# Opening of a silu MLP kernel: x's contraction tile 1 loaded behind the third warm-up matmul, first contraction tile multiplied by halves of the rows

## The chip, the cores and the metric

The kernel runs on one core of a Trainium2 chip. The metric is the device time of one execution in microseconds (us), where lower is better. The profile beside it was taken of one execution, and its span counts from the program's first instruction to its last.

## The reference

`x` is 2048 x 640, `w1` is 640 x 1728 and `w2` is 1728 x 640, all bf16.

```python
def reference(x, w1, w2):
    h = jnp.einsum("bsd,df->bsf", x, w1)
    h = _silu(h)
    out = jnp.einsum("bsf,fd->bsd", h, w2)
    return out
```

## The kernel before

The work is written out by hand as one list of operations. Each operation names its engine and the operations that it depends on; each engine runs its own operations in the order of that list, and a dependency on another engine or on a DMA becomes a semaphore wait in front of the instruction. Nothing is reordered by a planner.

TensorE (PE) needs x with its contraction dimension on the partitions. So x is held as `xT_sb`, five contraction tiles (`dt` 0 to 4) of 128 by 2048 rows. The rows are taken in four chunks of 512 (`SCH`). The first product is computed transposed: for each block `ft` of 128 columns of w1, five matmuls over `dt` accumulate 128 x 512 values in one PSUM bank; ScalarE (ACT) takes the sigmoid and VectorE (DVE) multiplies, which gives `hT_sb`. The second product (L326) reads `hT_sb` and `w2_sb`.

The change touches only the opening, up to the end of the first `column_group`:

- **Loads.** SP and ACT issue DMAs. Of x's first 512 rows, contraction tiles 0 and 1 arrive untransposed in `x0_sb` (`load_x0`, L144): tile 0 as two halves of the rows, `x0_a` on SP and `x0_b` on ACT, and tile 1 whole, `x0_c`, on ACT straight after `x0_b`. Tiles 2 to 4 arrive transposed by DMA (`transpose_x`, L152). The first six column blocks of w1 (`FA` = 6) arrive one contraction tile at a time, `w1_0` to `w1_4` (`load_w1`, L148, 192 KB each), followed by the rest, `w1_a` and `w1_b`. After its two DMAs ACT loads its function table and runs a first small sigmoid (L160).
- **Warm-up.** PE starts with matmuls of a constant (`warm_up`, L172), which use no data: five of 512 columns and one of 256, and after the transposes of tile 0 another 512 and 256.
- **Transposes of tile 0 and 1** (`transpose_x0`). Four PE transposes of 128 x 128 (L182) go to a PSUM bank. Tile 0 is copied to `xT_sb` by DVE in two halves of 256 rows (L186), tile 1 by ACT in one piece of 512 (L188).
- **First `column_group`** (L263). Six banks are filled side by side: for each `dt`, six matmuls of 512 columns, one per `ft`. The first of each `dt` waits for that tile's x and `w1_dt`. After the second matmul (`ft` = 1) of tile 0, the list has the four transposes of tile 1, so that four matmuls of 512 columns stand between them and the first matmul of tile 1. The last block of the group is followed by `unit` (L221), whose first matmul waits for `w1_a`.

Of the kernel before, what the change touches and what calls it, by code (L numbers as in the profile page):

```python
# [20 lines left out]
class Plan:  # L21
# [9 lines left out]
    def add(self, eng, emit, deps=(), group=None):  # L31
        op = Op(eng, emit, [d for d in deps if d is not None], group)
        self.ops.append(op)
        return op
# [40 lines left out]
def bass_standalone__dense_activation_silu__prompt_kernel(  # L75
# [6 lines left out]
    bf16 = mybir.dt.bfloat16  # L82
# [6 lines left out]
    P = 128  # L89
    H = P // 2  # L90
    SCH = 512
    DT = D // P
# [5 lines left out]
    JB = SCH // P  # L98
    NBANK = 8
# [3 lines left out]
    with ExitStack() as es:  # L103
        def sb(name, shape, dtype):
            return es.enter_context(nc.sbuf_tensor(name, shape, dtype))

        xT_sb = sb("xT_sb", [P, DT, S], bf16)
        w1_sb = sb("w1_sb", [P, DT, F], bf16)
# [5 lines left out]
        x0_sb = sb("x0_sb", [P, JB, D], bf16)  # L114
# [3 lines left out]
        ps = es.enter_context(nc.psum_tensor("ps", [P, NBANK, SCH], fp32))  # L118

        w1_v = w1.rearrange("(dt p) f -> p dt f", p=P)  # L120
        x0_v = xf[0:SCH, :].rearrange("(j p) d -> p j d", p=P)
# [3 lines left out]
        add = plan.add  # L125
        bank_free = [[] for _ in range(NBANK)]
        turn = [0]

        def take_bank():
            b = turn[0] % NBANK  # L130
            turn[0] += 1
            return b


        FA = 6
# [3 lines left out]
            out=ident[:, :], in_=ident[:, :], compare_op=ALU.not_equal, fill=1.0,  # L139
            base=0, pattern=[[-1, P]], channel_multiplier=1), [id_a])  # L140
        warm = add("dve", lambda e: e.memset(warm_sb[:, :], 0.0))

        def load_x0(eng, name, j0, j1, d0, d1):
            return add(eng, lambda e: e.dma_start(  # L144
                out=x0_sb[:, j0:j1, d0 * P:d1 * P], in_=x0_v[:, j0:j1, d0 * P:d1 * P]), group=name)

        def load_w1(eng, name, d0, d1, f0, f1, deps=()):
            return add(eng, lambda e: e.dma_start(  # L148
                out=w1_sb[:, d0:d1, f0:f1], in_=w1_v[:, d0:d1, f0:f1]), deps, group=name)

        def transpose_x(sc, dt, name, deps=()):
            return add("sp", lambda e: e.dma_start_transpose(  # L152
                out=xT_sb[:, dt, sc * SCH:(sc + 1) * SCH],
                in_=xf[sc * SCH:(sc + 1) * SCH, dt * P:(dt + 1) * P]), deps, group=name)

        x0_a = [load_x0("sp", "x0_a", 0, JB // 2, 0, 1), load_x0("act", "x0_b", JB // 2, JB, 0, 1)]
        w1_lo = [load_w1("sp", "w1_0", 0, 1, 0, FA * P)]
        x0_c = load_x0("act", "x0_c", 0, JB, 1, 2)
        w1_lo += [load_w1("sp", f"w1_{dt}", dt, dt + 1, 0, FA * P) for dt in (1, 2)]
        add("act", lambda e: e.activation(out=warm_sb[:, :], in_=warm_sb[:, :], func=ACT.Sigmoid), [warm])  # L160
        x0_t = {2: transpose_x(0, 2, "x0_2")}
# [3 lines left out]
        w1_dma = [load_w1("sp", f"w1_{name}", 0, DT, w1_cuts[g] * P, min(w1_cuts[g + 1] * P, F))  # L165
                  for g, name in enumerate("ab")]

        ones = nc.const_aps.tensor(1.0, [P, SCH], bf16)

        def warm_up(columns):  # L170
            for n in columns:
                add("pe", lambda e, n=n: e.matmul(  # L172
                    ps[:, NBANK - 1, 0:n], lhsT=ones[:, 0:P], rhs=ones[:, 0:n], start=True, stop=True))

        warm_up([SCH] * 5 + [2 * P])

        def transpose_x0(dt, j0, j1, b):

            dst = ps[:, b, :].bitcast(bf16)[:, j0 * P:j1 * P]
            out = xT_sb[:, dt, j0 * P:j1 * P]  # L180
            for j in range(j0, j1):
                t = add("pe", lambda e, j=j: e.transpose(  # L182
                    dst[:, (j - j0) * P:(j - j0 + 1) * P], x0_sb[:, j, dt * P:(dt + 1) * P], ident[:, :]),
                    [x0_a[j // (JB // 2)], id_b] if dt == 0 else [x0_c] + bank_free[b])
            if dt % 2 == 0:
                c = add("dve", lambda e: e.tensor_copy(out=out, in_=dst), [t])  # L186
            else:
                c = add("act", lambda e: e.copy(out=out, in_=dst), [t])  # L188
            bank_free[b] = [c]
            return c  # L190

        def x_deps(sc, c0, n):
            return x0T if sc == 0 else x1_of if sc == 1 else [x_dma[sc]]

        def w1_deps(ft):
            return [w1_dma[max(g for g in range(len(w1_dma)) if w1_cuts[g] <= ft)]] if ft >= FA else w1_lo
# [5 lines left out]
        def silu(b, parts, n, pe):  # L202
            s = sig_turn[0] % NSIG
            sig_turn[0] += 1
            a = add("act", lambda e: e.activation(  # L205
                out=sig_sb[:, s, 0:n], in_=ps[:, b, 0:n], func=ACT.Sigmoid), [pe, sig_free[s]])
            for rows, ft, cols in parts:
                v = add("dve", lambda e, rows=rows, ft=ft, cols=cols: e.tensor_tensor(  # L208
                    out=hT_sb[rows, ft, cols], in0=ps[rows, b, 0:n], in1=sig_sb[rows, s, 0:n],
                    op=ALU.mult), [a])  # L210
                chunk_done[cols.start // SCH] = v
                if ft == FR:
                    tail_done[cols.start // SCH] = v
            bank_free[b] = [v]
            sig_free[s] = v

        def unit(sc, ft, c0, n):
            b = take_bank()
            cols = slice(sc * SCH + c0, sc * SCH + c0 + n)
            for dt in range(DT):  # L220
                pe = add("pe", lambda e, dt=dt: e.matmul(  # L221
                    ps[:, b, 0:n], lhsT=w1_sb[:, dt, ft * P:(ft + 1) * P], rhs=xT_sb[:, dt, cols],
                    start=(dt == 0), stop=(dt == DT - 1)),
                    x_deps(sc, c0, n) + w1_deps(ft) + bank_free[b] if dt == 0 else ())
            silu(b, [(slice(0, P), ft, cols)], n, pe)

        def tail_unit(sc):
            b = take_bank()
            for dt in range(DT):
                for hh in range(2):  # L230
                    pe = add("pe", lambda e, dt=dt, hh=hh: e.matmul(  # L231
                        ps[hh * H:(hh + 1) * H, b, :], lhsT=w1_sb[:, dt, FR * P:F],
                        rhs=xT_sb[:, dt, (sc + hh) * SCH:(sc + hh + 1) * SCH],
                        start=(dt == 0), stop=(dt == DT - 1), skip_group_check=True),
                        x_deps(sc, 0, SCH) + x_deps(sc + 1, 0, SCH) + w1_deps(FR) + bank_free[b]
                        if dt == 0 else ())
            silu(b, [(slice(hh * H, (hh + 1) * H), FR, slice((sc + hh) * SCH, (sc + hh + 1) * SCH))
                     for hh in range(2)], SCH, pe)

        x_dma, x1_of, w2_dma = {}, [], []  # L240
        for sc in range(1, NSC):
# [4 lines left out]
            if sc == 2:  # L246
                half = FR // 2
                for a, z in ((0, half), (half, FR)):
                    w2_dma.append(add("sp", lambda e, a=a, z=z: e.dma_start(
                        out=w2_sb[:, a:z, :], in_=w2_v[:, a:z, :]), group="w2"))  # L250
                for hh in range(2):
                    w2_dma.append(add("sp", lambda e, hh=hh: e.dma_start(
                        out=w2_sb[hh * H:(hh + 1) * H, FR, :], in_=w2[FR * P:F, :]), group="w2"))

        def column_group(sc, x_dep, w1_dep, between=None):

            banks = [take_bank() for _ in range(FA)]
            for dt in range(DT):
                for ft in range(FA):
                    deps = bank_free[banks[ft]] if dt == 0 else []  # L260
                    if ft == 0:
                        deps = deps + [x_dep[dt], w1_dep[dt]]
                    pe = add("pe", lambda e, dt=dt, ft=ft: e.matmul(  # L263
                        ps[:, banks[ft], :], lhsT=w1_sb[:, dt, ft * P:(ft + 1) * P],
                        rhs=xT_sb[:, dt, sc * SCH:(sc + 1) * SCH],
                        start=(dt == 0), stop=(dt == DT - 1)), deps)
                    if dt == DT - 1:
                        silu(banks[ft], [(slice(0, P), ft, slice(sc * SCH, (sc + 1) * SCH))], SCH, pe)
                    if between and ft == 1:
                        between(dt + 1)  # L270

        def transpose_next(dt):
            if dt in x0_t:
                x0T.append(x0_t[dt])
            elif dt < DT:
                x0T.append(transpose_x0(dt, 0, JB, FA + dt % 2))

        half = [transpose_x0(0, k * JB // 2, (k + 1) * JB // 2, FA - 2 + k) for k in range(2)]
        x0T = [half[1]]
        warm_up([SCH, 2 * P])  # L280
        column_group(0, x0T, w1_lo, transpose_next)
        for ft in range(FA, FR):
            unit(0, ft, 0, SCH)

        for sc in range(1, NSC):
            if sc == 1:
                column_group(sc, x1_of, w1_lo)
            for ft in range(FA if sc == 1 else 0, FR):
                unit(sc, ft, 0, SCH)
        reg_done = dict(chunk_done)  # L290
# [111 lines left out]
```

## Time and profile before

| | us |
|---|---|
| median of three runs | 125.84 |
| lowest, highest | 125.55, 126.11 |
| profiled execution, time | 126.19 |
| profiled execution, span | 124.8 |
| PE busy | 121.7 (97% of the span) |
| DVE, ACT busy | 44.7, 38.8 |

The profiled execution lies 1.4 us above its own span and 0.35 us above the median of the three runs. A start or a duration below is counted in the span. Matmuls are pipelined: the record of one 512-column matmul is 379 ns long where the next one starts after 216 ns, so the spacing of starts tells the pace of PE, and the length of a record does not.

### The profile page before, as it was taken

What the parts mean: (1) busy time and instruction counts of PE and PEld (TensorE: products, weight loads), DVE (VectorE), ACT (ScalarE), POOL (GpSimd) and SP (SyncE); (2) the same over time, 40 slices, a digit from 0 to 9 for tenths busy, and PEclk for the clock granted to TensorE, in tenths of its full rate; (3) what the DMA queues carried; (4) which work ended last, traced back from release to release, by engine and by line L of the source; (5) the groups of instructions that cost most, each with busy time, mean ns of one, the idle gap of its engine ahead of it and who ended that gap; (6) DMA issues with size and microseconds to landing.
All of it is one profiled execution on the core that took longest, in us unless ns stands there. A gap on an engine that the chain in (4) does not pass through costs nothing.

```text
span 124.8 us, 2074 instructions
## 1 busy us (share of the span) xinstructions
PE 121.7 (97%) x890; PEld 57.1 (46%) x890; DVE 44.7 (36%) x70; ACT 38.8 (31%) x68; POOL 0.7 (1%) x6
## 2 busy tenths in 40 slices
PE   7999999999999999999999999999999999999992
PEld 2444444444444444444444444444444444446481
DVE  0102984079666666666682020202021020202021
ACT  4104953097555555555530010101011010101021
POOL 2000000000000000000000000000000000000000
PEclk9999999999999999999999999999999999999999
DMA  3989682559980000000000001115120201102434
GB/s 69 293 179 347 141 102 54 114 100 373 349 170 3 0 5 0 3 0 0 0 0 5 0 2 30 26 21 181 39 105 5 105 0 21 33 15 74 158 104 112
DMA packets 20201, 10.41 MB, mean 83 GB/s; under 512 B 14432, under 2 KB 20192, under 8 KB 20192
## 3 DMA queue, kind: packets, MB, share of 16 engines
q1 hardware_dynamic: 19104, 9.95, 30.0%
q10 hardware_dynamic: 1088, 0.33, 1.1%
q8 instruction: 7, 0.11, 0.4%
q14 instruction: 2, 0.02, 0.1%
HBM read 4.77 MB, written 2.62 MB: 59 GB/s over the span
## 4 chain that ended last, share of the span: by engine, by line
PE 98%; DVE 0%; issue 0%
PE ps L326 47%; PE ps L221 35%; PE ps L263 11%; PE ps L172 3%; PE ps L231 2%; PE ps L182 1%; DVE o_sb L337 0%
## 5 line engine op out<-in xcount | busy, mean ns | idle before, releaser
L326 PE MATMUL ps<-w_sb,hT_sb 64*128 64x512 bf16 (+2 forms) x486 | 47.3, 352 | 0.0
L208 DVE TENSOR_TENSOR hT_sb<-ps,sig_sb 128x512 bf16<-128x512 f32 (+1 forms) x56 | 37.0, 688 | 25.3 <-ACT sig_sb L205 25.3
L221 PE MATMUL ps<-xT_sb,w_sb 128*128 128x512 bf16 x200 | 43.5, 379 | 0.0
L205 ACT ACTIVATE sig_sb<-ps 128x512 bf16<-128x512 f32 x54 | 30.7, 606 | 27.5 <-PE ps L221 16.4
L326 PEld LDWEIGHTS ps<-w_sb,hT_sb 64*128 64x128 bf16 x486 | 23.5, 94 | 23.5
L221 PEld LDWEIGHTS ps<-xT_sb,w_sb 128*128 128x128 bf16 x200 | 19.6, 98 | 23.6
L337 DVE CAST o_sb<-ps 128x512 bf16<-128x512 f32 (+2 forms) x9 | 5.7, 632 | 37.6 <-PE ps L326 37.6
L339 ACT CAST o_sb<-ps 128x512 bf16<-128x512 f32 (+2 forms) x9 | 4.8, 538 | 38.6 <-PE ps L326 38.6
L263 PE MATMUL ps<-xT_sb,w_sb 128*128 128x512 bf16 x60 | 14.1, 392 | 0.0
L326 PE MATMUL ps<-hT_sb,w_sb 64*128 64x512 bf16 x108 | 12.3, 376 | 0.0
L263 PEld LDWEIGHTS ps<-xT_sb,w_sb 128*128 128x128 bf16 x60 | 5.9, 101 | 7.4 <-DVE xT_sb L186 0.7
L326 PEld LDWEIGHTS ps<-hT_sb,w_sb 64*128 64x128 bf16 x108 | 5.2, 94 | 6.5 <-issue 0.4
L337 DVE CAST oT_sb<-ps 128x512 bf16<-128x512 f32 x2 | 1.4, 692 | 11.7 <-PE ps L326 11.7
L339 ACT CAST oT_sb<-ps 128x512 bf16<-128x512 f32 x2 | 1.2, 585 | 13.6 <-PE ps L326 13.6
L172 PE MATMUL ps<-const-bfloat16-1.0 128*128 128x512 bf16 (+1 forms) x8 | 3.4, 575 | 0.8 <-PEq L387 0.8
L231 PE MATMUL ps<-xT_sb,w_sb 128*64 128x512 bf16 x20 | 2.3, 381 | 0.0
L172 PEld LDWEIGHTS ps<-const-bfloat16-1.0 128*128 128x128 bf16 x8 | 1.0, 140 | 1.8 <-issue 1.8
L160 ACT ACT_TABLE_LOAD x1 | 1.3, 1283 | 1.8 <-issue 1.8
L231 PEld LDWEIGHTS ps<-xT_sb,w_sb 128*64 128x64 bf16 x20 | 1.0, 110 | 1.2 <-issue 0.4
L186 DVE COPY xT_sb<-ps 128x256 bf16<-128x256 bf16 x2 | 0.5, 292 | 2.6 <-PE ps L182 2.6
L182 PEld LDWEIGHTS ps<-ident,x_sb 128*128 128x128 bf16 x8 | 1.0, 144 | 0.9 <-DMA x_sb<-in_x_dram 0.6
L188 ACT COPY xT_sb<-ps 128x512 bf16<-128x512 bf16 x1 | 0.6, 585 | 2.5 <-PE ps L182 2.5
(9 smaller groups left out, 2.5 us busy)
## 6 DMA issues: line engine op xcount, KB each, us to landing
out_dram<-o_sb SPq DMA_DIRECT2D x14, 160.0 KB, 1.9
w_sb<-in_w_dram SPq DMA_DIRECT2D x1, 1120.0 KB, 7.7
w_sb<-in_w_dram SPq DMA_DIRECT2D x5, 192.0 KB, 3.1
w_sb<-in_w_dram SPq DMA_DIRECT2D x1, 960.0 KB, 5.6
w_sb<-in_w_dram SPq DMA_DIRECT2D x1, 880.0 KB, 5.5
w_sb<-in_w_dram SPq DMA_DIRECT2D x1, 320.0 KB, 3.7
xT_sb<-in_x_dram SPq DMA_TRANSPOSE x18, 3.0
o_sb<-oT_sb SPq DMA_TRANSPOSE x16, 2.3
```

The lines of the kernel that those rows point to most:

```text
L160: add("act", lambda e: e.activation(out=warm_sb[:, :], in_=warm_sb[:, :], func=ACT.Sigmoid), [warm])
L172: add("pe", lambda e, n=n: e.matmul(ps[:, NBANK - 1, 0:n], lhsT=ones[:, 0:P], rhs=ones[:, 0:n], start=True, stop=True))
L182: t = add("pe", lambda e, j=j: e.transpose(dst[:, (j - j0) * P:(j - j0 + 1) * P], x0_sb[:, j, dt * P:(dt + 1) * P], ident[:, :]), [x0_a[j ...
L188: c = add("act", lambda e: e.copy(out=out, in_=dst), [t])
L205: a = add("act", lambda e: e.activation(out=sig_sb[:, s, 0:n], in_=ps[:, b, 0:n], func=ACT.Sigmoid), [pe, sig_free[s]])
L208: v = add("dve", lambda e, rows=rows, ft=ft, cols=cols: e.tensor_tensor(out=hT_sb[rows, ft, cols], in0=ps[rows, b, 0:n], in1=sig_sb[rows, ...
L221: pe = add("pe", lambda e, dt=dt: e.matmul(ps[:, b, 0:n], lhsT=w1_sb[:, dt, ft * P:(ft + 1) * P], rhs=xT_sb[:, dt, cols], start=(dt == 0), ...
L231: pe = add("pe", lambda e, dt=dt, hh=hh: e.matmul(ps[hh * H:(hh + 1) * H, b, :], lhsT=w1_sb[:, dt, FR * P:F], rhs=xT_sb[:, dt, (sc + hh) * ...
L263: pe = add("pe", lambda e, dt=dt, ft=ft: e.matmul(ps[:, banks[ft], :], lhsT=w1_sb[:, dt, ft * P:(ft + 1) * P], rhs=xT_sb[:, dt, sc * SCH:( ...
L326: pe = add("pe", lambda e, b=b, n=n, lhsT=lhsT, rhs=rhs, ft=ft: e.matmul(ps[:, b, 0:n], lhsT=lhsT, rhs=rhs, start=(swap == 0 and ft == 0), ...
L337: ev = add("dve", lambda e, b=b, n=n, dst=dst: e.tensor_copy(out=dst, in_=ps[:, b, 0:n]), [pe])
L339: ev = add("act", lambda e, b=b, n=n, dst=dst: e.copy(out=dst, in_=ps[:, b, 0:n]), [pe])
```

## The change

ACT's DMA of x's tile 1 (`x0_c`) now waits for the third warm-up matmul; for that, the warm-up matmuls stand ahead of the loads in the list, which leaves PE's own order as it was. The warm-up behind the transposes of tile 0 keeps only its matmul of 256 columns. The first contraction tile of the first `column_group` is multiplied as twelve matmuls of 256 columns, first all six blocks on the first 256 rows, and then all six on the other 256; the first half waits only for the first half's copy. The transposes of tile 1 come after the second block of the second half. Tile 1's copy moves from ACT to DVE. The transposes of tile 0 use banks 6 and 7 in place of 4 and 5, and the warm-up bank 0 in place of 7.

```diff
+        early = warm_up([SCH] * 3)
+        warm_up([SCH] * 2 + [2 * P])
...
-        x0_c = load_x0("act", "x0_c", 0, JB, 1, 2)
+        x0_c = load_x0("act", "x0_c", 0, JB, 1, 2, [early])
...
-        warm_up([SCH] * 5 + [2 * P])
...
-            if dt % 2 == 0:
+            if dt < 2:
                 c = add("dve", lambda e: e.tensor_copy(out=out, in_=dst), [t])
             else:
                 c = add("act", lambda e: e.copy(out=out, in_=dst), [t])
...
             banks = [take_bank() for _ in range(FA)]
             for dt in range(DT):
-                for ft in range(FA):
-                    deps = bank_free[banks[ft]] if dt == 0 else []
-                    if ft == 0:
-                        deps = deps + [x_dep[dt], w1_dep[dt]]
-                    pe = add("pe", lambda e, dt=dt, ft=ft: e.matmul(
-                        ps[:, banks[ft], :], lhsT=w1_sb[:, dt, ft * P:(ft + 1) * P],
-                        rhs=xT_sb[:, dt, sc * SCH:(sc + 1) * SCH],
-                        start=(dt == 0), stop=(dt == DT - 1)), deps)
...
+                parts = len(x_dep[dt])
+                for h in range(parts):
+                    c0, c1 = h * (SCH // parts), (h + 1) * (SCH // parts)
+                    for ft in range(FA):
+                        deps = [x_dep[dt][h], w1_dep[dt]] if ft == 0 else []
+                        if dt == 0 and h == 0:
+                            deps = deps + bank_free[banks[ft]]
+                        pe = add("pe", lambda e, dt=dt, ft=ft, h=h, c0=c0, c1=c1: e.matmul(
+                            ps[:, banks[ft], c0:c1], lhsT=w1_sb[:, dt, ft * P:(ft + 1) * P],
+                            rhs=xT_sb[:, dt, sc * SCH + c0:sc * SCH + c1],
+                            start=(dt == 0 and h == 0), stop=(dt == DT - 1), skip_group_check=True), deps)
...
+                        if between and h == parts - 1 and ft == 1:
+                            between(dt + 1)
...
-        half = [transpose_x0(0, k * JB // 2, (k + 1) * JB // 2, FA - 2 + k) for k in range(2)]
-        x0T = [half[1]]
-        warm_up([SCH, 2 * P])
+        half = [transpose_x0(0, k * JB // 2, (k + 1) * JB // 2, FA + k) for k in range(2)]
+        x0T = [half]
+        warm_up([2 * P])
         column_group(0, x0T, w1_lo, transpose_next)
```

More of the change, by code (lines that the diff above doesn't have):

```diff
@@ L141, in bass_standalone__dense_activation_silu__prompt_kernel, with warm_up, load_x0 @@
         warm = add("dve", lambda e: e.memset(warm_sb[:, :], 0.0))
-        def load_x0(eng, name, j0, j1, d0, d1):
+        ones = nc.const_aps.tensor(1.0, [P, SCH], bf16)
+        def warm_up(columns):
+            for n in columns:
+                last = add("pe", lambda e, n=n: e.matmul(
+                    ps[:, 0, 0:n], lhsT=ones[:, 0:P], rhs=ones[:, 0:n], start=True, stop=True))
+            return last
+        early = warm_up([SCH] * 3)
+        warm_up([SCH] * 2 + [2 * P])
+        def load_x0(eng, name, j0, j1, d0, d1, deps=()):
             return add(eng, lambda e: e.dma_start(
-                out=x0_sb[:, j0:j1, d0 * P:d1 * P], in_=x0_v[:, j0:j1, d0 * P:d1 * P]), group=name)
+                out=x0_sb[:, j0:j1, d0 * P:d1 * P], in_=x0_v[:, j0:j1, d0 * P:d1 * P]), deps, group=name)
         def load_w1(eng, name, d0, d1, f0, f1, deps=()):
@@ L166, in bass_standalone__dense_activation_silu__prompt_kernel @@
                   for g, name in enumerate("ab")]
[L168 to L173, printed above, removed]
-        warm_up([SCH] * 5 + [2 * P])
         def transpose_x0(dt, j0, j1, b):
@@ L192, in x_deps @@
         def x_deps(sc, c0, n):
-            return x0T if sc == 0 else x1_of if sc == 1 else [x_dma[sc]]
+            return x0T[-1] if sc == 0 else x1_of if sc == 1 else [x_dma[sc]]
         def w1_deps(ft):
@@ L258, in column_group @@
             for dt in range(DT):
-                for ft in range(FA):
-                    deps = bank_free[banks[ft]] if dt == 0 else []
-                    if ft == 0:
-                        deps = deps + [x_dep[dt], w1_dep[dt]]
-                    pe = add("pe", lambda e, dt=dt, ft=ft: e.matmul(
-                        ps[:, banks[ft], :], lhsT=w1_sb[:, dt, ft * P:(ft + 1) * P],
-                        rhs=xT_sb[:, dt, sc * SCH:(sc + 1) * SCH],
-                        start=(dt == 0), stop=(dt == DT - 1)), deps)
[L267 to L270, printed above, removed]
+                parts = len(x_dep[dt])
@@ new lines, in column_group @@
+                for h in range(parts):
[8 more added lines that the diff above has]
+                            start=(dt == 0 and h == 0), stop=(dt == DT - 1), skip_group_check=True), deps)
+                        if dt == DT - 1:
+                            silu(banks[ft], [(slice(0, P), ft, slice(sc * SCH, (sc + 1) * SCH))], SCH, pe)
+                        if between and h == parts - 1 and ft == 1:
+                            between(dt + 1)
@@ L272, in transpose_next @@
         def transpose_next(dt):
             if dt in x0_t:
-                x0T.append(x0_t[dt])
+                x0T.append([x0_t[dt]])
             elif dt < DT:
-                x0T.append(transpose_x0(dt, 0, JB, FA + dt % 2))
-        half = [transpose_x0(0, k * JB // 2, (k + 1) * JB // 2, FA - 2 + k) for k in range(2)]
-        x0T = [half[1]]
-        warm_up([SCH, 2 * P])
+                x0T.append([transpose_x0(dt, 0, JB, FA + dt % 2)])
+        half = [transpose_x0(0, k * JB // 2, (k + 1) * JB // 2, FA + k) for k in range(2)]
@@ L286, in bass_standalone__dense_activation_silu__prompt_kernel @@
             if sc == 1:
-                column_group(sc, x1_of, w1_lo)
+                column_group(sc, [[d] for d in x1_of], w1_lo)
             for ft in range(FA if sc == 1 else 0, FR):
```

## The prediction

> **What bounds the kernel now.** I read the chain of waits first. It is one engine, PE, from start to end:
>
> ```profile
> by line: PE ps L326 46.9%; PE ps L221 34.6%; PE ps L263 11.0%; PE ps L172 2.5%; PE ps L231 1.8%; PE ps L182 0.7%; DVE o_sb L337 0.3%; issue 0.1%
> ...
> 0.77 2.51 PE ps L172 x6
> 3.28 0.43 PE ps L182 x4
> 3.71 0.64 PE ps L172 x2
> 4.35 0.00 issue
> 4.35 1.01 PE ps L263 x2
> 5.36 0.43 PE ps L182 x4
> 5.79 6.27 PE ps L263 x28
> 12.06 7.55 PE ps L221 x35
> ```
>
> Two things are to be seen. From 4.35 us on PE never waits, so the end of the program moves by what the opening moves. And the pace changes: L221 runs 35 matmuls in 7.55 us, 0.216 each, while the first two of L263 take twice that. The timeline gives the starts:
>
> ```profile
> 1.26 1.40 SPq L148 DMA_DIRECT2D w_sb<-in_w_dram  x3
> ...
> 3.07 0.63 PE L182 MATMUL ps<-ident,x_sb 128*128 128x128 bf16 x4
> ...
> 3.50 0.85 PE L172 MATMUL ps<-const-bfloat16-1.0 128*128 128x512 bf16 x2
> 3.53 0.51 DVE L186 COPY xT_sb<-ps 128x256 bf16<-128x256 bf16 x2 [2.63 <-PE ps L182]
> ...
> 4.32 0.14 PEld L263 LDWEIGHTS ps<-xT_sb,w_sb 128*128 128x128 bf16 x2 [0.67 <-DVE xT_sb L186]
> ...
> 5.16 0.63 PE L182 MATMUL ps<-ident,x_sb 128*128 128x128 bf16 x4
> ...
> 5.83 0.58 ACT L188 COPY xT_sb<-ps 128x512 bf16<-128x512 bf16 x1 [2.50 <-PE ps L182]
> ```
>
> Slow, a 512-column matmul is spaced 0.427 (the transposes, a quarter as wide, 0.107). After the transposes at 5.16 the group's third matmul starts at 5.58, and L221's first at 11.90: 28 matmuls in 6.32 us, of which 28 x 0.216 = 6.05 would be needed. The surplus of 0.27 is 1.3 slow matmuls, so the step to double pace lies near 6.13. The granted clock reads 1.00 in every stretch and does not show it; the spacing does.
>
> Then, what ended the wait before 4.32? The row names DVE, but DVE's second copy was over at 3.53 + 0.51 = 4.04. The landings say otherwise; for `w1_0`, issued at 1.26, and for `x0_c`, issued at 1.27:
>
> ```profile
> L148 SPq DMA_DIRECT2D w_sb<-in_w_dram x1: 447/447/447, 1.3 to 1.3; - x1
> ...
> DMA to landing us min/median/max: 3.0/3.0/3.0
> ```
>
> ```profile
> L144 ACTq DMA_DIRECT2D x_sb<-in_x_dram x1: 502/502/502, 1.3 to 1.3; - x1
> ...
> DMA to landing us min/median/max: 3.3/3.3/3.3
> ```
>
> `w1_0` landed at 4.21, and the matmul began 0.14 later. Warm-up ended (by spacing) at 3.50 + 0.43 + 0.21 = 4.14. So the start at 4.35 is `w1_0`'s. `x0_c` landed at 4.60; PE wanted it at 5.16.
>
> **The change part by part.** All times are in the profiled execution (126.19 us, 0.35 above the median of the runs); the sum is a shift, which I then put on the median.
>
> *Less warm-up.* One slow matmul, 0.427 us, goes: PE is ready for the group at 3.71, not 4.14. By itself it is worth nothing, since `w1_0` is later than either.
>
> *`x0_c` later.* The third warm-up starts at 1.58 and its record ends at 2.21; PE's end reaches another engine 0.04 later (transposes' end 3.49, copy's start 3.53), so ACT issues at 2.25, 1 us later than now. Behind the wait on ACT stand the table load (1.28) and the small sigmoid, which then end near 4.3; ACT's first needed work is at 11.02, so this is free. SP's queue is untouched.
> For `w1_0`, the sixteen parts of its landing came between 3.49 and 4.21, fifteen by 3.99, while 256-byte packets of `x0_c` ran from 3.05 to 4.15. Bounds: issue to landing not under the 2.3 of `x0_b` (3.56), not over the present 3.0 (4.21). I take 3.95, the fifteenth part. First matmul = the later of that + 0.14 and of DVE's first half (3.82 + some 0.1): 4.09, between 3.93 and 4.35. The gain at this place is 0.26.
> [...]
> `x0_c` itself: 2.25 plus 2.3 to 3.3 gives 4.55 to 5.6. Tile 1's transposes now come after eight matmuls of 256 columns, 4.09 + 8 x 0.213 = 5.80. Covered, by 0.2 to 1.2. What `x0_c` now collides with, `w1_1` and `w1_2`, landed at 5.10 and 5.82 and is wanted at about 6.7 and 8.0.
>
> *Halves.* 3072 slow columns cost the same in twelve pieces as in six. Six more weight loads of 0.15 hide behind matmuls spaced 0.213; if they did not, 6 x 0.15 would be the ceiling, but transposes spaced 0.107 already hide such loads. Zero.
>
> *The transposes of tile 1 move back in the work, and their copy loses its cover.* This is the term that decides. Now: transposes, then four matmuls of 512 columns (2048 columns) hide their result latency and ACT's 0.58 copy, which is over at 6.41; the first matmul of tile 1 starts at 6.72, by spacing (5.58 + 0.43 + 0.27 + 2 x 0.216). After: only four of 256 columns (1024) are left behind them. The path: last transpose starts 5.80 + 3 x 0.107 = 6.12, its record is 0.31, then 0.04, then DVE's copy, then 0.09 to the matmul (between the 0.04 and 0.14 seen behind landings). DVE's copy of 128 x 512 bf16 is not in the trace:
>
> ```profile
> L337 DVE CAST o_sb<-ps 128x512 bf16<-128x512 f32 x7 | 4.8, 692 | 34.8 <-PE ps L326 34.8
> ...
> L186 DVE COPY xT_sb<-ps 128x256 bf16<-128x256 bf16 x2 | 0.5, 292 | 2.6 <-PE ps L182 2.6
> ...
> L337 DVE CAST o_sb<-ps 128x320 bf16<-128x320 f32 x1 | 0.5, 493 | 2.2 <-PE ps L326 2.2
> ```
>
> The f32 rows differ by 199 ns for 192 columns: 1.04 a column, and 160 fixed. The bf16 row is 292 = 160 + 132 for 256, half of that a column. So 512 cost 160 + 264 = 0.42; the upper bound is 0.56 (the second half at 1.04). I take 0.42. Sum: 6.12 + 0.31 + 0.04 + 0.42 + 0.09 = 6.98. PE itself would be ready at about 6.6 (transposes to 6.2, 1024 fast columns 0.43), so 0.35 us of new idle time. Against 6.72 that is **+0.26 us**. With a start at 3.93 it is +0.10; with 4.35, +0.45 (part of it then at the fast pace); 0.56 for the copy adds 0.14.
>
> In short: the 0.26 gained at the start is spent at half pace (worth 0.13), and the uncovered copy costs 0.39. From tile 1 on, everything is as before; x's tiles 2 to 4 landed 1 us or more before use, and `w1_a`, which landed at 11.24 for a weight load at 11.68, gets more room. Forecast: 125.84 + 0.26 = 126.1 us.
>
> **The rivals.**
>
> *A: the step to double pace does not stand at 6.13.* One profile shows one execution. If the step comes later, the copy is covered by slow matmuls and the earlier start counts in full: wholly slow, before needs 4.35 + 3584 x 0.833 ns = 7.34 to reach tile 1, after 4.09 + 2.99 = 7.08, or -0.26 (-0.41 from 3.93). That gives 125.4 to 125.6. Break-even is a step near 6.6. For it: the runs differ by 0.56 us, which some such thing must explain. Against: the profiled execution, slower than all three, should have the latest step, and its copy is uncovered. Chance 0.25.
> [...]
>
> *B, slower: idle time on PE puts the step off.* PE now idles 0.21 between warm-up and group; after, 3.71 to 4.09, 0.38, or 0.64 if `w1_0` is no earlier. If that restarts whatever grants the pace, the step comes as long after 4.09 as it now comes after 0.77: 5.36 later, at 9.45. The 3.3 us between run at half pace, half of them lost: +1.6, and 127.5. It decides from a gap somewhere above 0.21. Against: the present gap did not restart it. Chance 0.09.
> [...] No run here shows a longer gap.
>
> *C: `x0_c` comes too late.* If the collision with `w1_1` and `w1_2` adds half a microsecond to its longest case, it lands at 6.1, transposes start at 6.15, 0.35 late: 126.45, up to 126.8. From 5.7 on it decides. Chance 0.10.
>
> *D: the change does not do what it says:* `w1_0` lands at 4.2 regardless, held by something other than `x0_c`. Start 4.35, +0.45: 126.3. Chance 0.12.
>
> **How the numbers follow.** Forecast 0.44, A 0.25, B 0.09, C 0.10, D 0.12. A's lower side and the runs' spread put the lower end at 125.4, C's the upper at 126.8; B, part of C and the extremes of A stay outside. Half a percent, 0.63 us, is about what a measurement of this kernel can tell from no change: faster by more needs A's extreme plus something, 0.08; slower by more is B, most of C and the tail of D, 0.19; the rest is the same, 0.73.
>
> **What would show it.** Right: L263's first matmul at 4.0 to 4.2; `w1_0` landing under 4.1; a new wait of the weight load on DVE's copy (512 columns, near 0.42) before tile 1, and tile 1's first matmul at 6.8 to 7.1 if the step stays near 6.1. Wrong: no such wait, a step off by half a microsecond or more, or transposes that wait for `x0_c`.

## The result, and the profile after

The changed kernel takes 126.94 us (median of four runs, 126.86 to 127.03) against 125.69 for the kernel before beside it: a ratio of 1.0083, 95% interval 1.0058 to 1.0108. The two medians differ by 1.25 us; the ratio stands for 1.04. The forecast was 126.1 with a range up to 126.8; the kernel is slower than that. Ratios leave out runs over 1.5% above the fastest of their kernel, which are seven of the twelve in e6, so that there the median tells more. The profiled execution took 126.86 with a span of 125.5, 0.7 longer than before.

The chain of waits, which was PE alone before, now reads (start us, us, what):

```profile
by line: PE ps L333 46.6%; PE ps L223 34.4%; PE ps L270 9.4%; DMA x_sb<-in_x_dram 3.4%; PE ps L233 1.8%; PE ps L147 1.2%; DVE xT_sb L188 0.3%; PE ps L184 0.3%; DVE o_sb L344 0.3%; issue 0.2%
...
0.78 1.45 PE ps L147 x3
2.23 0.02 issue
2.25 4.29 DMA x_sb<-in_x_dram
6.54 0.05 issue
6.58 0.41 PE ps L184 x4
6.99 0.02 issue
7.02 0.44 DVE xT_sb L188
7.45 0.05 issue
7.50 5.35 PE ps L270 x24
```

To be seen: the chain leaves PE after the third warm-up matmul, goes through ACT's DMA `x0_c` for 4.29 us, then through the transposes of tile 1 and DVE's copy, and is back on PE at 7.50, where tile 1 starts. Before, that was at 6.72. All of the difference between these two executions is there: 0.78 us at this point, and from here on the two chains run alike. (It is less than the 1.04 of the ratio because the profiled execution before, with 126.19, lies above the runs' median.)

The timeline after, for the same places as before:

```profile
2.25 0.42 ACTq L155 DMA_DIRECT2D x_sb<-in_x_dram  x1
...
3.50 0.42 PE L147 MATMUL ps<-const-bfloat16-1.0 128*128 128x256 bf16 x1
...
4.08 1.45 PE L270 MATMUL ps<-xT_sb,w_sb 128*128 128x256 bf16 x8 [0.16 <-DVE xT_sb L188]
...
6.58 0.40 PE L184 MATMUL ps<-ident,x_sb 128*128 128x128 bf16 x4 [1.05 <-DMA x_sb<-in_x_dram]
...
7.02 0.42 DVE L188 COPY xT_sb<-ps 128x512 bf16<-128x512 bf16 x1 [2.98 <-PE ps L184]
7.50 0.55 PEld L270 LDWEIGHTS ps<-xT_sb,w_sb 128*128 128x128 bf16 x4 [0.36 <-DVE xT_sb L188]
```

The eight half matmuls start at 4.08 and are done, by spacing, at 5.37; the transposes start at 6.58. That is 1.21 us in which PE has nothing to do (1.05 in the bracket, since the record of the last half matmul ends at 5.53, 0.16 later). Then tile 1 waits for the copy: the last half matmul is through by 7.25, the next starts at 7.50.

The balance up to tile 1, in this execution. Idle time of PE: 0.37 (3.71 to 4.08) + 1.21 + 0.25 = 1.83 against 0.21, so +1.62. One warm-up matmul less, -0.43. PE's work from the group's start to tile 1 took 7.50 - 4.08 - 1.21 - 0.25 = 1.96 against 2.37, -0.41, because the step to double pace came near 4.98 (the matmul at 4.89 is followed by one at 5.04, between the slow spacing of 0.213 and the fast one of 0.109) and not at 6.13. Together +0.78.

### The profile page after: what moved, and what is told of

Same layout as the page of the kernel before. It is cut to its first block, busy times and chain, and to the rows that moved or that the text cites. A ratio compares the mean times of both kernels' runs of the same rounds, so it can differ in the third digit from the quotient of the medians.

```text
span 125.5 us, 2084 instructions
## 1 busy us (share of the span) xinstructions
PE 121.2 (97%) x895; PEld 57.0 (45%) x895; DVE 45.2 (36%) x71; ACT 38.3 (31%) x67; POOL 0.7 (1%) x6
## 4 chain that ended last, share of the span: by engine, by line
PE 94%; DMA 3%; DVE 1%; issue 0%
PE ps L333 47%; PE ps L223 34%; PE ps L270 9%; DMA x_sb<-in_x_dram 3%; PE ps L233 2%; PE ps L147 1%; DVE xT_sb L188 0%; PE ps L184 0%; DVE o_sb L344 0%
## 5 line engine op out<-in xcount | busy, mean ns | idle before, releaser
L223 PE MATMUL ps<-xT_sb,w_sb 128*128 128x512 bf16 x200 | 43.5, 379 | 0.0
L223 PEld LDWEIGHTS ps<-xT_sb,w_sb 128*128 128x128 bf16 x200 | 19.6, 98 | 23.6
L270 PE MATMUL ps<-xT_sb,w_sb 128*128 128x512 bf16 (+1 forms) x66 | 14.0, 369 | 0.2 <-DVE xT_sb L188 0.2
L270 PEld LDWEIGHTS ps<-xT_sb,w_sb 128*128 128x128 bf16 x66 | 6.5, 101 | 7.3 <-DVE xT_sb L188 0.9
L147 PE MATMUL ps<-const-bfloat16-1.0 128*128 128x512 bf16 (+1 forms) x7 | 2.9, 566 | 0.8 <-PEq L394 0.8
L188 DVE COPY xT_sb<-ps 128x256 bf16<-128x256 bf16 (+1 forms) x3 | 0.9, 336 | 5.6 <-PE ps L184 5.6
L184 PE MATMUL ps<-ident,x_sb 128*128 128x128 bf16 x8 | 1.0, 268 | 1.1 <-DMA x_sb<-in_x_dram 1.1
```

Source lines behind the costliest of these rows:

```text
L147: last = add("pe", lambda e, n=n: e.matmul(ps[:, 0, 0:n], lhsT=ones[:, 0:P], rhs=ones[:, 0:n], start=True, stop=True))
L184: t = add("pe", lambda e, j=j: e.transpose(dst[:, (j - j0) * P:(j - j0 + 1) * P], x0_sb[:, j, dt * P:(dt + 1) * P], ident[:, :]), [x0_a[j ...
L223: pe = add("pe", lambda e, dt=dt: e.matmul(ps[:, b, 0:n], lhsT=w1_sb[:, dt, ft * P:(ft + 1) * P], rhs=xT_sb[:, dt, cols], start=(dt == 0), ...
L270: pe = add("pe", lambda e, dt=dt, ft=ft, h=h, c0=c0, c1=c1: e.matmul(ps[:, banks[ft], c0:c1], lhsT=w1_sb[:, dt, ft * P:(ft + 1) * P], rhs= ...
```

## The experiments

The medians, each with that of the kernel before measured beside it; `x0_c` and `w1_0` (start of the issue and landing, us) as in the one profiled execution of each:

| run | median us, before | ratio (95%) | `x0_c` issued, landed | `w1_0` landed |
|---|---|---|---|---|
| before | | | 1.27, 4.60 | 4.21 |
| after | 126.94, 125.69 | 1.0083 (1.0058 to 1.0108) | 2.25, 6.54 | 3.95 |
| e5, after again | 126.94, 125.98 | 1.0064 (1.0041 to 1.0087) | 2.25, 6.69 | 4.21 |
| e1, no wait | 126.23, 126.25 | 1.0009 (0.998 to 1.0037) | 1.25, 4.42 | 3.93 |
| e2, wait only | 127.36, 126.25 | 1.0062 (1.004 to 1.0084) | 2.25, 6.26 | 4.67 |
| e3, second warm-up | 126.17, 126.25 | 0.9998 (0.9975 to 1.0022) | 1.82, 5.51 | 4.09 |
| e4, cover | 126.12, 126.25 | 0.9992 (0.9977 to 1.0008) | 1.27, 4.57 | 4.04 |
| e6, tile 2 later | 128.61, 125.98 | 1.008 (1.0043 to 1.0116) | 2.25, 7.04 | 3.76 |
| e7, no second warm-up | 126.16, 125.98 | 1.0 (0.9982 to 1.0018) | 1.25, 4.98 | 4.52 |
| e8, cover and `w1_a` on ACT | 126.59, 125.98 | 1.0042 (1.0024 to 1.0061) | 1.27, 4.57 | 3.89 |
| e9, `x0_c` on SP | 126.55, 126.04 | 1.0047 (1.0028 to 1.0066) | 1.75, 4.57 | 4.03 |
| e10, cover and `w1_1`, `w1_2` on ACT | 126.27, 126.04 | 1.0024 (0.9999 to 1.0049) | 1.26, 4.82 | 4.01 |
| e11, before and `w1_1`, `w1_2` on ACT | 126.55, 126.04 | 1.0038 (1.002 to 1.0056) | 1.25, 4.54 | 3.92 |

**Which part of the change costs the time: e1 and e2.** e1 takes the wait out of the changed kernel:

```diff
-        x0_c = load_x0("act", "x0_c", 0, JB, 1, 2, [early])
+        x0_c = load_x0("act", "x0_c", 0, JB, 1, 2)
```

> The changed kernel without the wait of x0_c on the third warm-up matmul; halves, transposes' place and shorter warm-up stay. Theory L (the late landing of x0_c is nearly all of the loss): x0_c lands near 4.6 as in the kernel before, w1_0 near 4.2, so the first matmul of the group starts at 4.35; no wait for x0_c; what is left is the uncovered copy of tile 1: a wait of 0.2 to 0.45 us on DVE ahead of tile 1, and 0.1 to 0.45 us more than the kernel before, 125.8 to 126.2. Rival H (the halves or the shorter warm-up cost the time): the loss of about 1.1 us stays, 126.8 to 127.

e2 puts the wait alone into the kernel before (the first six warm-up matmuls listed ahead of the loads, as in the change):

```diff
-        x0_c = load_x0("act", "x0_c", 0, JB, 1, 2)
+        x0_c = load_x0("act", "x0_c", 0, JB, 1, 2, [early])
```

> The kernel before with one thing of the change: x0_c waits for the third warm-up matmul. Theory L: x0_c lands near 6.5, its transposes start at 6.6 in place of 5.2, after them four fast matmuls of 512 columns (0.86 us) against ACT's copy path of 0.22 + 0.04 + 0.59 + 0.05 on top of 6.76: tile 1 starts near 7.7, about 1 us later than before, so 126.6 to 127.0. Rival H: as the kernel before, 125.5 to 125.9.

Without the wait the loss is gone (1.0009, an interval on both sides of 1), with the wait alone it is there (1.0062; five of its twelve runs lie near 127.4, two at 128.5). So the wait is the cause, and halves, shorter warm-up and the copy's move to DVE together cost nothing that can be told here. Two expectations of e1 were off: `w1_0` landed at 3.93 without any delay of `x0_c`, not at 4.2, and its profile has no wait for the copy of tile 1 (the step came at 6.78, so slow matmuls covered it).

e2's profile is of an execution of 128.45 us. Tile 1 starts there at 8.42 and not near 7.7, because the step comes only at 10.1: PE idled 0.67 us ahead of the group (4.14 to 4.81) and 0.69 us ahead of tile 1's transposes (5.62 to 6.31), and ran at half pace for 5.3 us after the group's start. That is what rival B of the prediction describes (5.36), in a kernel that keeps the whole warm-up.

**The changed kernel again: e5.** Nothing is edited.

> The changed kernel itself, unaltered, to have it beside the others on one chip. Theory L (its end is set by x0_c's landing, which does not depend on where the step to double pace falls): 0.6 to 1.2 us above the kernel before, a narrow spread, PE waiting about 1 us for x0_c, which lands 4.0 to 4.3 after its issue. Rival: the first difference of 0.83% was an accident of the chip; then within 0.3 us of the kernel before.

1.0064, with six of seven runs between 126.54 and 127.17 and one at 128.57. In its profile the step to double pace came before the group's first matmul, at 4.27, and yet tile 1 started at 7.65: once PE is ready early, `x0_c`'s landing at 6.69 sets the start of tile 1, with an early step as with a later one. In this execution the copy was waited for as well, and the transposes started 1.5 us after PE was through with the halves.

**Why `x0_c` lands so late: e3, e6, e9.** e3 moves the wait to the second warm-up matmul:

```diff
-        early = warm_up([SCH] * 3)
-        warm_up([SCH] * 2 + [2 * P])
+        early = warm_up([SCH] * 2)
+        warm_up([SCH] * 3 + [2 * P])
```

> The changed kernel with x0_c behind the second warm-up matmul in place of the third: it is issued near 1.83 in place of 2.25 (1.27 before). Theory T (x0_c becomes late only when its landing falls in with the DMA transposes of x's tile 2, whose packets start near 4.7): its data is through before them, it lands 3.2 to 3.4 after its issue, 5.0 to 5.3, PE does not wait for it or by under 0.1 us, and the time is 125.8 to 126.3. Rival W (w1_1 and w1_2 in front of it take the DMA engines, so that lateness grows evenly with the delay): landing between 4.6 and 6.54 in proportion, 5.7 or 5.8, PE waits 0.2 to 0.4 us, 126.2 to 126.5.

It landed 3.7 after its issue, at 5.51: midway between the two theories. PE did not wait, because the group started at 4.23 and wanted it only at 5.89; the time is that of the kernel before.

e6 moves SP's first transposes out of `x0_c`'s way:

```diff
-        x0_t = {2: transpose_x(0, 2, "x0_2")}
-        for dt in (3, 4):
-            w1_lo.append(load_w1("sp", f"w1_{dt}", dt, dt + 1, 0, FA * P))
+        w1_lo.append(load_w1("sp", "w1_3", 3, 4, 0, FA * P))
+        w1_lo.append(load_w1("sp", "w1_4", 4, 5, 0, FA * P))
+        x0_t = {}
+        for dt in (2, 3, 4):
             x0_t[dt] = transpose_x(0, dt, f"x0_{dt}")
```

> The changed kernel with SP's three DMA transposes of x's tiles 2 to 4 moved behind w1_3 and w1_4, so that their packets start near 5.7 in place of 5.0, after x0_c's; x0_c's wait stays. Theory T (x0_c is late because its landing falls in with the first DMA transposes): x0_c lands by 5.7, PE waits for it at most 0.2 us, the time falls by 0.5 to 0.9 us against the changed kernel. Rival W (the copies of w1 take the engines; there are now two more of them beside x0_c): x0_c lands at 6.4 or later, the time does not fall.

Theory T falls as the whole of the cause: with the transposes moved back and two more copies of w1 close behind it, `x0_c` landed later still, at 7.04, 4.8 after its issue. The edit changes two things at once, though, so it does not show that the transposes add nothing.

e9 takes the other way, an issue about as late as in e3, with `w1_1` and `w1_2` behind it in one queue:

```diff
-        x0_c = load_x0("act", "x0_c", 0, JB, 1, 2, [early])
+        x0_c = load_x0("sp", "x0_c", 0, JB, 1, 2)
```

> The changed kernel with x0_c issued by SP between w1_0 and w1_1, near 1.75, with no wait. Issue is then about as late as in the run behind the second warm-up matmul (1.82, landed 5.51), and the one difference is that w1_1 and w1_2 stand behind x0_c in SP's queue in place of ahead of it. Theory W (the w1 copies issued ahead of x0_c make it late, not the delay itself): it lands 2.8 to 3.1 after its issue, at 4.6 to 4.9, no wait for it on PE, and the time is that of the kernel before within 0.4 us; w1_a lands up to 0.5 later, since all behind x0_c on SP moves by one issue. Rival (any later issue lands this late): 5.3 to 5.7.

The instructions of the loading line, first e3's `x0_c` and then e9's (start, and time from issue to landing):

```profile
L155 ACTq DMA_DIRECT2D x_sb<-in_x_dram x1: 398/398/398, 1.8 to 1.8; - x1
...
DMA to landing us min/median/max: 3.7/3.7/3.7
```

```profile
L155 SPq DMA_DIRECT2D x_sb<-in_x_dram x1: 427/427/427, 1.8 to 1.8; - x1
...
DMA to landing us min/median/max: 2.8/2.8/2.8
```

Issued within 0.07 us of each other, one took 3.7 and the other 2.8. That is as theory W had it: not the delay as such, but what was issued ahead of `x0_c` and is still being moved. The thirteen profiles taken together go the same way. With no copy of w1 but `w1_0` ahead, `x0_c` takes 2.8 to 3.7 (eight profiles; the longest are e10 with 3.6 and e7 with 3.7), behind `w1_1` 3.7 (e3), behind `w1_1` and `w1_2` 4.0 to 4.4 (e2, after, e5), and with `w1_3` and `w1_4` close behind as well 4.8 (e6). Two things keep this from being shown outright. e7's 3.7 is as long as e3's, so one pair of profiles proves little; and e9, the only run that parts a later issue from more copies ahead, also moved `x0_c` from ACT's queue to SP's.

The time of e9 missed its expectation: 1.0047. In the profile there is no wait for any DMA; only `w1_b`, pushed back by one issue on SP, landed at 14.23, 0.09 before it was wanted (10 matmuls of 0.216 after 12.16). Executions with an earlier step would want it sooner; e4 and e7 below, whose steps were early, do wait for theirs, which landed at 13.95 and 13.82. That such waits are e9's loss is likely, and no profile of e9 shows it.

**The copy's cover: e4.** e1 with the transposes of tile 1 after the fourth matmul of the first half:

```diff
-                        if between and h == parts - 1 and ft == 1:
+                        if between and h == 0 and ft == (3 if parts == 2 else 1):
```

> As the run without the wait, and the transposes of tile 1 come after the fourth matmul of the first half of the rows, so that eight matmuls of 256 columns (2048 columns, as before) stand between them and tile 1. Theory C (the copy of tile 1 lost its cover): the wait on DVE ahead of tile 1 goes, and the time is that of the kernel before within 0.15 us, 0.15 to 0.45 us under the run without the wait. Rival: the uncovered copy cost nothing, both runs agree.

The wait on the copy is gone (tile 1 follows at the usual spacing, at 6.10), as expected. The gain over e1 cannot be told: 126.12 against 126.23, with overlapping intervals. And e4's lead did not reach the end. Its chain, shortened:

```profile
6.37 1.12 SPq L163
7.53 4.09 DMA w_sb<-in_w_dram
11.62 0.05 issue
11.67 7.89 PE ps L223 x35
```

With tile 1 at 6.10, PE was ready for `w1_a` 0.39 us before its first matmul could start at 11.67, and the chain goes back through SP's queue, where six copies and three transposes of 1.1 to 1.2 us of issue each stand ahead of it. Its first matmul with `w1_a` is still 0.23 us ahead of the kernel before, where L221 started at 11.90, but the next load takes most of that: `w1_b` landed at 13.95, PE was ready for it at 13.83 and started with it at 13.99. At 19.56 the chain is 0.05 us ahead of the kernel before (19.61). The same shows in e7, the kernel before without its second warm-up, whose profile had an early step: PE was ready for `w1_b` at 13.51 and started with it at 13.96:

```profile
8.17 5.66 DMA w_sb<-in_w_dram
13.82 0.14 issue
13.96 5.56 PE ps L221 x25
```

Its lead of 0.55 us at L221's first matmul (11.35) is down to 0.1 at 19.52. So `w1_a` (landed at 11.62 in e4) and `w1_b` (13.95 in e4, 13.82 in e7), behind all the other loads of the opening in SP's queue, are a floor under it. In these two executions the floor lay 0.05 and 0.1 us below the profiled kernel before; where `w1_b` lands at 13.61, as in that one, it would lie some 0.3 to 0.4 below (an estimate: landing + 0.04 to 0.14, as here, against the start at 14.05).

**Lifting the floor: e8, e10, e11.** e8 is e4 with 512 warm-up columns behind tile 0's transposes and `w1_a` issued by ACT once tile 1 is copied:

```diff
+                w1_dma[0].deps.append(x0T[-1][0])
...
-        warm_up([2 * P])
+        warm_up([SCH])
...
-        w1_dma = [load_w1("sp", f"w1_{name}", 0, DT, w1_cuts[g] * P, min(w1_cuts[g + 1] * P, F))
+        w1_dma = [load_w1(("act", "sp")[g], f"w1_{name}", 0, DT, w1_cuts[g] * P, min(w1_cuts[g + 1] * P, F))
```

> A version meant to be faster: halves without the wait of x0_c, tile 1's transposes after the fourth matmul of the first half, the warm-up behind the transposes of 512 columns, and w1_a issued by ACT once tile 1 is copied in place of by SP in eighth place (it ended a wait of 0.23 us at 11.67 in the run with the cover). Expected: no wait for w1_a, tile 1 started at 6.0 to 6.6 according to the step, 0.1 to 0.5 us under the kernel before. Rival: w1_a now takes the DMA engines from w1_4 and x's tile 4, and PE waits for one of them before their matmuls; then no gain.

The rival came true. From its chain:

```profile
6.34 4.68 DMA xT_sb<-in_x_dram
11.06 1.04 PE ps L270 x4
```

x's tile 4 took 4.68 us to land (2.96 before) with `w1_a` beside it, and PE waited 0.43 us for it: a load that took longer beside another, as `x0_c` did. e10 is e4 with `w1_1` and `w1_2` on ACT, and e11 the kernel before with that alone:

```diff
-        w1_lo += [load_w1("sp", f"w1_{dt}", dt, dt + 1, 0, FA * P) for dt in (1, 2)]
+        w1_lo += [load_w1("act", f"w1_{dt}", dt, dt + 1, 0, FA * P) for dt in (1, 2)]
```

> A version meant to be faster: the run with the cover, with w1_1 and w1_2 issued by ACT behind x0_c in place of by SP. SP is then through with its transposes 0.9 us sooner, and w1_a lands that much earlier, near 10.7. Theory: PE does not wait for w1_a, and the time is 0.2 to 0.4 us under the run with the cover, which waited 0.39 us for w1_a. Rival: tile 2's transposes, now earlier, fall in with x0_c, which lands at 5 or later, PE waits for it, no gain or a loss of up to 0.5.

> The kernel before with that same move alone, w1_1 and w1_2 issued by ACT behind x0_c. If the gain of the run beside it comes from SP's earlier end, this one gains 0.1 to 0.3 us too in executions with an early step and nothing in the others; if it comes from the halves and the cover, this one is as the kernel before.

In e10 `w1_a` landed at 10.46 (and `w1_b` at 12.77) and nothing waited for them, but the time is not better, 1.0024. e11 is slower, 1.0038. Both profiles have a late step (6.74 and 6.68) and no wait for a DMA; what the other executions wait for stays open. No version here beats the kernel before.

**Idle time and the step: e7.** The kernel before without the two warm-up matmuls behind tile 0's transposes:

```diff
-        warm_up([SCH, 2 * P])
```

> The kernel before without the two warm-up matmuls behind the transposes of tile 0, nothing else: PE idles from 3.50 to the start of the group, 0.55 to 0.85 us in place of about 0.2. Theory G (idle time in the opening can put the step to double pace off by a whole period): some of the runs lie 1.3 to 1.8 us above the others, and where the profile shows such an execution its step comes near 9 to 10 us in place of 4.9 to 6.8; the rest are as the kernel before. Rival: the step does not mind the gap, all runs lie within 0.6 us of the kernel before's median.

Eleven of twelve runs lie between 125.67 and 126.33, one at 127.65; the ratio is 1.0. In the profiled execution PE idled from 3.50 to 4.66 (`w1_0` at 4.52) and then ran at double pace at once. So the warm-up that the change shortens was worth nothing in the middle of the runs. Single late runs are another matter. In the kernels with a shorter second warm-up or none and no late `x0_c` (e1, e3, e4, e7, e9, e10) five of 72 runs lie 1.2 to 1.5 us above their kernel's median; in those with at least 512 columns of it (before, e8, e11) none of 121 does, and the highest of the kernel before is 0.63 above. That fits theory G, but none of the five was profiled. What came after idle time is seen in e2's profile (above) and in e6's. By windows (the stretch, its span in us, busy time and count of PE, PEld, DVE, ACT and POOL, granted clock, DMA share, GB/s):

```profile
0.77:4.14 3.37, 3.37 (x13) 1.48 (x14) 0.59 (x3) 1.44 (x2) 0.46 (x2) 1.00 0.62 152
4.14:7.55 3.41, 1.36 (x15) 1.00 (x14) 0.03 (x1) 0.08 (x1) 0.00 (x0) 1.00 1.10 291
7.55:10.97 3.42, 3.42 (x12) 1.16 (x10) 0.40 (x1) 0.00 (x0) 0.00 (x0) 0.50 0.73 192
10.97:14.38 3.41, 3.40 (x16) 1.56 (x16) 0.00 (x0) 0.62 (x2) 0.00 (x0) 1.00 0.88 278
```

In the second stretch PE was busy for only 1.36 of 3.41 us, most of the rest waiting for `x0_c`. In the third the granted clock is 0.50, and 512-column matmuls are spaced 0.427 again. That is the price of rival B, 3.42 us at half pace or 1.7 us, beside the wait of rival C. It would account for part of the spread of e6's runs, from 126.05 to 130.66, of which only this one was profiled.

## Why the prediction was right or wrong

The sign was right and the size was not: +0.26 us forecast, +1.0 measured (0.83% of 125.84), with a median 0.14 above the upper end of the range. That the sign fits is luck: it was to come from the uncovered copy, and it came from `x0_c`, which the forecast had on time. The profile shows what the prediction itself named as a sign of being wrong, transposes that wait for `x0_c`. Point by point:

- **What bounds the kernel before** held: from tile 1 on, the shift at tile 1 is the shift of the end (0.78 in the profiles, of which the span shows 0.7). It holds for a shift to later. A shift to earlier was mostly swallowed by `w1_a` and `w1_b` in e4 and e7, so a gain in the opening need not reach the end.
- **`x0_c`'s landing is the step that failed.** "2.25 plus 2.3 to 3.3 gives 4.55 to 5.6. ... Covered, by 0.2 to 1.2." It took 4.29, so PE, which was ready at 5.37, waited 1.21 us. The two ends came from rows in which this transfer or a like one was ahead of `w1_1` and `w1_2`; here it was issued after them: its packets ran from 4.21 to 6.08, `w1_1` and `w1_2` landed at 4.44 and 5.68, and the DMA share was 1.05, 0.92, 1.06 and 1.15 in four stretches (2.25 to 3.25, 4.20, 5.15 and 6.10). That the wait makes `x0_c` late and that this is the loss is shown by e1 and e2; that it is the copies ahead of it that hold it up rests on the thirteen landings above and on e9, and is likely rather than shown. The prediction named that collision, asked only what it does to `w1_1` and `w1_2`, and gave `x0_c`'s side to rival C with a chance of 0.10 and half a microsecond. Rival C was the outcome, twice as large: from 5.7 on it decides, as said, and the landing was at 6.54, not 6.1, since 1.0 and not 0.5 came on top of the longest case of 3.3.
- **`w1_0` sooner without `x0_c`**: 3.95 was taken and 3.95 measured, which is luck, as the reason given does not hold. In the five profiles with a wait `w1_0` landed at 3.76 to 4.67, median 4.09; in the eight without at 3.89 to 4.52, median 4.02. What the wait was to bring cannot be seen. The row that suggested it was one execution's late sixteenth part. (The packets of `x0_c` in that row ran from 3.15 to 4.26, not from 3.05 to 4.15; nothing hangs on it.) The transfer that took longer was the other one: `x0_c`, from ACT, took 4.29 among SP's copies, against 3.3 before.
- **Start of the group**: 4.09 forecast, 4.08 measured in the first profile, 4.35 in e5.
- **DVE's copy of 512 columns**: 0.42 forecast, and the row by form says 425 ns:

```profile
L188 DVE COPY xT_sb<-ps 128x512 bf16<-128x512 bf16 x1 | 0.4, 425 | 3.0 <-PE ps L184 3.0
```

- **The uncovered copy** was the term that was to decide. It is there, 0.25 of waiting against 0.35 forecast, and only where the step is early: e1's profile, with the step at 6.78, has none. Behind a wait of 1.21 it does not decide, and e1 against e4 could not show it in the times.
- **Halves at no cost**: e1, which has them together with the shorter warm-up and DVE's copy, bears that out within its interval of -0.2 to +0.4%.
- **Rival A, the step anywhere**: right about the step, which ought to have been part of the forecast rather than a rival; the gain that it was to bring did not come. In eleven of the thirteen profiles the step lies between 4.1 and 6.8, in e7 between 3.5 and 4.7, in e2 at 10.1. e5 shows that an early step no longer helps once `x0_c` sets the start of tile 1.
- **Rival B**: not in the profiled executions of the changed kernel, whose gaps ahead of the group were 0.37 and 0.64 (after, e5). It happened in the profiled execution of e2 (step at 10.1 after two gaps of 0.7 us) and, once PE had been at full pace, in e6's. If the five high runs above are the same, it comes in about one run in fifteen of kernels with a shorter second warm-up.

## What to carry to other kernels

A transfer that is issued later may also take longer (`x0_c`: 3.3 us issued at 1.27, 4.29 at 2.25): price it with what will by then be in flight, not with the duration that it had in its old place; where it comes from another queue than the loads beside it, try the order in one queue (2.8 us in e9, 3.7 in e3), and count what it pushes back (in e9 `x0_c` came in time and `w1_b` landed at 14.23, against 13.61 before). Before a load is delayed in favour of another, look at several executions to see whether the other was held up by it at all. Before an opening is made shorter, look for the load that ends up as its floor. A wait in the opening can be paid twice, once as idle time and once more as a stretch at half pace (in e6 2.05 us without a PE record, and then 3.42 us at a granted clock of 0.50).

## What the runs showed of the hardware

- The records of the granted clock give a full-speed stretch of 119.466 us in the kernel before (from 6.13), e1 (6.78), e3 (6.11) and e4 (5.01), and of 122.880 in e5 (from 4.27), which is 3.414 longer. In e6 the clock reads 0.50 for 3.42 us (7.55 to 10.97), between stretches at 1.00. The first warm-up matmul starts at 0.77 in the kernel before and in e1, and the full-speed stretch 5.36 and 6.01 after it.
- At full pace, 2.05 us without a PE record (e6, 4.14 to 7.55) were followed by a stretch at half clock; a wait of 1.4 us for `x0_c` (e5, 1.5 by spacing) was not, and the mean granted clock of that execution is 1.0. At half pace, 0.35 us without a PE record (e5, up to 4.27) were followed by full speed; after gaps of 0.67 and 0.69 us by spacing (e2, 4.14 to 4.81 and 5.62 to 6.31) full speed came only at 10.1. What sets these cases apart is not shown.
- In the kernel before, the granted clock reads 1.00 in every stretch from 0.50 on, while its first record starts at 6.13 and 512-column matmuls were spaced 0.427 before that; the spacing shows its slow opening, and that column does not.
- The sixteen parts of `x0_c` did not land together: in the profile after, fifteen had landed by 5.93 and the last came at 6.54. The transfer's data was late there too: nine tenths of its 512 packets had started by 5.19, and the last ended at 6.08. What held that part is open.
